# Token halves exchanged in half of the heads of an mLSTM kernel, so that the four quarters of TensorE's array get equal columns

## The chip, the cores and the metric

The kernel runs on one core of one Trainium2 chip. A core has a matrix engine (TensorE, PE in the profile, with PEld for its weight loads), VectorE (DVE), ScalarE (ACT), GpSimd (POOL), a queue that only issues transfers (SyncE, SP), and 16 DMA engines. The metric is the device time of one execution in microseconds; times below are the median of three runs.

## The reference

Two blocks follow each other. The first is an mLSTM cell, a recurrence with exponential gates over 768 tokens, for 4 batches and 8 heads of 40 dimensions:

```python
for t in range(S):
    m_new = np.maximum(f_gate[:, :, t] + m, i_gate[:, :, t])
    f_stab = np.exp(f_gate[:, :, t] + m - m_new)
    i_stab = np.exp(i_gate[:, :, t] - m_new)
    C = f_stab * C + i_stab * einsum('bhd,bhe->bhde', vt, kt)
    n = f_stab * n + i_stab * kt
    h_tilde, nq = einsum('bhde,bhe->bhd', C, qt), einsum('bhd,bhd->bh', n, qt)
    y[:, :, t] = sigmoid(o_gate) * h_tilde / np.maximum(np.abs(nq), 1.0)
```

The second, a mixture of depths, scores each token of the result (320 numbers), picks the 128 best of each batch, and adds a gated two-layer network for those alone:

```python
xe = x[b, top_idx]
ye = np.maximum(xe @ w1, 0.0) @ w2          # 320 -> 1024 -> 320
out[b, top_idx] = x[b, top_idx] + sigmoid(scores[b, top_idx])[:, None] * ye
```

## The kernel before

The recurrence is done in chunks. A tile is 128 tokens of one batch; there are 6 a batch, 24 in all, and `step(n)` handles tile n while it prepares tiles n+1 and n+2. Within a tile every pair of tokens (s, t) with s not after t gives a product k.q times a weight; earlier tiles come in through the state C.

For a tile, TensorE does this:

- `turn` (L314) transposes k and q, so that heads stand on partitions: two heads of 64 (40 used) fill the 128.
- `products` (L371) multiplies k by q. One head takes 64 rows of the array, and 64 tokens of k take 64 columns, so each product lies in one quarter of the array. For the first 64 tokens of k all 128 tokens of q are needed, for the last 64 only the last 64 of q, since the others come before them. Each matmul in float32 shows as two records.
- `weights` (L347, in the first tile L343 and L345) makes the exponents of the weights from two operands, a (from the input gate and the forget gate's sums) by k's token and M (a running maximum) by q's token. ScalarE takes their exponential (L348).
- `exchange` (L397, L403) applies the state C to q, and multiplies k by the weighted v, for the next state. `within` (L428) multiplies the weighted products P by v.

GpSimd's `causal` (L353) sets the weights of pairs in the wrong order to zero, in two selects of four heads each; in the first tile a matrix of large negative numbers, `never` (L332), does it instead. DVE multiplies products and weights to P (L377), adds the state's share to `within` (L433), makes the denominators (L437 to L441), and multiplies by the gate into x (L448), which is stored. GpSimd makes sor, the gate over the denominator (L443), wv, the weighted v (L360), and the decayed C (L385).

The gates come first. They lie as 96 rows (3 tiles, 4 batches, 8 heads) of 128 tokens, in two groups of three tiles. `sums` and `maxima` are scans on DVE (L194, L198). `split` (L230 to L233) cuts a row of float32 into three bfloat16 parts, which TensorE then spreads over partitions (pO: L272, L247): `split(g, 1, ...)` does a, `split(g, 0, ...)` does M. `scales` (L236, L237) makes the factors that weight v and the state, `columns` and `keep` turn them (L282, L287).

Each engine executes its instructions in the order in which the Python text issues them: that order is written out by hand, first for the tiles 0 to 3, then in `step`. So an instruction that waits holds up all that stand behind it on its engine. A transfer that ScalarE, SyncE or GpSimd issues stands in that engine's queue too. Transfers issued by SyncE and ScalarE share eight semaphores: each waits until the transfer that used its semaphore before, eight earlier, has landed.

Loads are issued four tiles ahead, at the start of a step, into five buffers. From step 8 on the network of the batch before is done in pieces in each step: `first` (L546), `second` (L570), and `enter` (L526), which transposes the rows that an indirect transfer (`gather`, L510) has fetched by the numbers that `number` (L503) makes. The weights w1 and w2 are loaded in six pieces, one a step after the steps 7 to 12. The last batch's choice, gather and network come after the last step, one behind the other.

The step's order around the network is this (L698 to L709):

```python
W[n + 2] = weights(*steps[n + 2]); hide(n + 2)   # hide: causal
layer(b, c)                                      # c == 1: layers[b - 2].second(3, 6)
if c == 1:
    picked[b - 1] = gather(b - 1, number(sel[b - 1], token))
elif c == 2:
    enter(b - 1)
```

Of the kernel before, what the change touches and what calls it, by code (L numbers as in the profile page):

```python
# [8 lines left out]
FP = mybir.dt.float32  # L9
BF = mybir.dt.bfloat16  # L10
# [11 lines left out]
def kernel(  # L22
# [61 lines left out]
    def load_gates(eng, dst, src, g):  # L84
        for c in range(3):
# [20 lines left out]
                            channel_multiplier=-1)  # L106
    ident_b = const.tile([128, 128], BF, name="ident_b")
# [14 lines left out]

    def load_qk(n):
        for j, src in enumerate((k, q)):
            load_heads(n, qk_t[n % NB][:, j, :, 0:D], src)

    def load_v(n):
        load_heads(n, v_t[n % NB][:, :, 0:D], v)
# [17 lines left out]

    def places(u, js=(0, 1)):
        for j in js:
            own, sign = ((0, -1.0), (3, 1.0))[j]
            for part in range(3):  # L150
                nc.gpsimd.tensor_scalar(out=place[j][u][:, part, :, own + part, :], op0=OP.mult, scalar1=sign, scalar2=None,
                                        in0=head[:, 16 * u:16 * u + 16].rearrange("p (g h) -> p g h", h=4))
# [6 lines left out]
    for j in range(2):  # L159
        nc.vector.tensor_reduce(out=of[:, j:j + 1], op=OP.add, axis=AX.XY,  # L160
                                in_=ident.rearrange("p (g x) -> p g x", x=32)[:, :, 12 * j:12 * j + 12])
    nc.vector.tensor_reduce(out=third, in_=ident[0:NR, 0:NR].rearrange("p (c h) -> p c h", h=BH), op=OP.add, axis=AX.X)
# [10 lines left out]
    a = [gate.tile([NR, L], FP, name=f"a{g}") for g in range(2)]  # L173
    m_in = [gate.tile([NR, 1], FP, name=f"m_in{g}") for g in range(2)]
# [22 lines left out]
    def maxima(g):  # L197
        nc.vector.tensor_tensor_scan(out=FM[g][:, 1], data0=ones, data1=a[g], initial=-BIG, op0=OP.mult, op1=OP.max)  # L198

# [27 lines left out]
    def split(g, j, eng, rows=slice(0, NR)):  # L227
        x, xs = (FM[g][rows, 1], a[g][rows])[j], [part[rows] for part in parts[j][g]]
        rest = gate.tile([NR, L], FP, name=f"rest{j}", bufs=2)[rows]
        eng.tensor_copy(out=xs[0], in_=x)  # L230
        eng.tensor_tensor(out=rest, in0=x, in1=xs[0], op=OP.subtract)
        eng.tensor_copy(out=xs[1], in_=rest)
        eng.tensor_tensor(out=xs[2], in0=rest, in1=xs[1], op=OP.subtract)  # L233

    def scales(g):
        nc.scalar.activation(out=wk[g], in_=a[g], func=AF.Exp, bias=nM[g], scale=1.0)  # L236
        nc.scalar.activation(out=r[g], in_=FM[g][:, 1], func=AF.Exp, bias=m_in[g], scale=-1.0)  # L237
# [90 lines left out]
    def masked(pools):  # L328

        pW = [pool.tile([128, 4, L], FP, name="pW", tag=tag) for pool, tag in pools]  # L330
        for p in pW:
            nc.tensor.matmul(p, never, ident_b.unsqueeze(1).to_broadcast([128, 4, L]), start=True, stop=False)  # L332
# [18 lines left out]
    def causal(W):  # L351
        for h0 in range(0, H, 4):
            nc.gpsimd.affine_select(out=W[:, h0:h0 + 4, :], in_=W[:, h0:h0 + 4, :], compare_op=OP.is_ge, fill=0.0, base=0,  # L353
                                    pattern=[[0, 4], [1, L]], channel_multiplier=-1)
# [9 lines left out]
    def products(T):  # L364
# [3 lines left out]
        for p in range(NP):  # L368
            for s, ts in zip(HALVES, (slice(0, L), HALVES[1])):
# [274 lines left out]
    def step(n):  # L644
# [52 lines left out]
        else:  # L697
# [7 lines left out]
            layer(b, c)  # L705
            if c == 1:
                picked[b - 1] = gather(b - 1, number(sel[b - 1], token))
            elif c == 2:
                enter(b - 1)  # L709
# [39 lines left out]
    maxima(0)  # L749
    split(0, 1, nc.gpsimd)  # L750
# [18 lines left out]
    split(1, 1, nc.gpsimd)  # L769
# [9 lines left out]
    maxima(1)  # L779
    stated(0)  # L780
# [12 lines left out]
    stated(1)  # L793
    iota_i = const.tile([128, K_], I32, name="iota_i")
# [9 lines left out]
    level(1, pm)  # L804
    split(1, 0, nc.gpsimd)
# [49 lines left out]
    for n in range(3, N):  # L855
# [6 lines left out]
        if 0 <= n - NT - 1 < 6:  # L862
            piece = n - NT - 1
# [80 lines left out]
```

## Time and profile before

| | |
|---|---|
| median of three runs | 182.86 us (182.71 to 184.8) |
| profiled execution | 184.28 us |
| its span, first to last instruction | 181.3 us, granted clock 0.998 |
| PE, PEld | 169.9 us (94%), 140.1 us (77%) busy |
| DVE, ACT, POOL | 135.8 us (75%), 102.1 us (56%), 105.8 us (58%) |
| DMA | 24.68 MB, 106,801 packets, 100,752 of them under 512 B |
| load of k, q, v or the gate of a tile | 160 KB each, 4.0 to 4.9 us from issue to landing (medians) |
| products L371 | 768 matmul records, half of 128 columns and half of 64 |
| causal L353 | 46 selects, 678 ns each in the mean |

In the profile a group names a line, an engine and an operation, then "out<-in"; `x48` is its count, and behind the bar stand the busy time, the mean of one in ns, and the time that the engine sat idle just before, with what ended most of that. In a timeline the first number is the start and the second the length, in us, and a bracket gives the idle time before and its releaser. SPq and ACTq are transfers issued by SyncE and ScalarE. In the chain each row is a start, a length and what the end of the program waited for at that time. A matmul's length includes the time in which it passes through the array, so the next one starts before it ends, and a busy PE isn't PE at its peak.

### The profile page before, as it was taken

What the parts mean: (1) busy time and instruction counts of PE and PEld (TensorE: products, weight loads), DVE (VectorE), ACT (ScalarE), POOL (GpSimd) and SP (SyncE); (2) the same over time, 40 slices, a digit from 0 to 9 for tenths busy, and PEclk for the clock granted to TensorE, in tenths of its full rate; (3) what the DMA queues carried; (4) which work ended last, traced back from release to release, by engine and by line L of the source; (5) the groups of instructions that cost most, each with busy time, mean ns of one, the idle gap of its engine ahead of it and who ended that gap; (6) DMA issues with size and microseconds to landing.
All of it is one profiled execution on the core that took longest, in us unless ns stands there. A gap on an engine that the chain in (4) does not pass through costs nothing.

```text
span 181.3 us, 7327 instructions
## 1 busy us (share of the span) xinstructions
PE 169.9 (94%) x2992; PEld 140.1 (77%) x2992; DVE 135.8 (75%) x403; ACT 102.1 (56%) x250; POOL 105.8 (58%) x176
## 2 busy tenths in 40 slices
PE   7989997999999999999989899999999999989990
PEld 2578976878777878889778598898878979869950
DVE  7767888898888875968996669698988788584120
ACT  3186869899998896466634454565535652201100
POOL 7987987778887992526854543655666361013202
PEclk9999999999999999999999999999999999999999
DMA  3999999999998999999999999889962101010100
GB/s 72 153 148 138 155 158 179 180 171 177 166 160 164 229 179 224 194 160 236 143 208 208 193 175 176 154 167 173 160 68 76 40 36 40 36 40 36 38 0 36
DMA packets 106801, 24.68 MB, mean 136 GB/s; under 512 B 100752, under 2 KB 106512, under 8 KB 106768
## 3 DMA queue, kind: packets, MB, share of 16 engines
q1 hardware_dynamic: 105952, 22.77, 77.6%
q0 software_dynamic: 384, 1.31, 2.5%
q8 instruction: 23, 0.38, 1.0%
q10 hardware_dynamic: 432, 0.15, 0.6%
q14 instruction: 10, 0.08, 0.2%
HBM read 19.63 MB, written 4.59 MB: 134 GB/s over the span
## 4 chain that ended last, share of the span: by engine, by line
PE 61%; issue 12%; ACT 10%; DMA 7%; POOL 5%; DVE 3%; POOLq 1%
PE pH L428 10%; PE ph L546 10%; PE pS L371 10%; PE pt L314 8%; PE pIC L397 5%; DMA xe<-out_dram,idx 5%; PE pIC L403 4%; PE pW L347 3%; PE py L570 3%; PE pS L190 3%; ACT W L348 2%; ACT M_o L258 2%; POOL W L353 2%; ACT T L315 2%; DMA out_dram<-ye,idx 2%
## 5 line engine op out<-in xcount | busy, mean ns | idle before, releaser
L443 POOL TENSOR_TENSOR sor<-so,rec 128x320 f32<-128x320 f32 x24 | 17.8, 740 | 36.7 <-DVE rec L441 32.7
L348 ACT ACTIVATE W<-pW 128x512 f32<-128x512 f32 x48 | 26.1, 598 | 20.8 <-PE pW L347 20.5
L377 DVE TENSOR_TENSOR P<-pS,W 128x512 f32<-128x512 f32 x48 | 30.9, 686 | 3.6 <-PE pS L371 1.6
L315 ACT COPY T<-pt 128x512 f32<-128x512 f32 x47 | 25.3, 589 | 12.8 <-PE pt L314 12.3
L353 POOL TENSOR_SCALAR_AFFINE_SELECT W<-W 128x512 f32<-128x512 f32 x46 | 30.2, 678 | 3.2 <-ACT W L348 3.2
L428 PEld LDWEIGHTS pH<-v,P 128*64 128x64 f32 x768 | 24.4, 138 | 8.6 <-DVE x L448 3.5
L428 PE MATMUL pH<-v,P 128*64 128x64 f32 x768 | 27.6, 225 | 2.5 <-issue 1.3
L471 DVE SCALAR_TENSOR_TENSOR ge<-sb,sc,earlier 128x128 bf16<-128x128 f32 (+5 forms) x23 | 18.1, 792 | 13.0 <-ACT sb L465 12.9
L371 PE MATMUL pS<-T 64*64 64x64 f32 (+1 forms) x768 | 26.2, 255 | 0.0
L314 PE MATMUL pt<-ident,qk 128*128 128x128 f32 x192 | 25.6, 276 | 0.2 <-ACT W L348 0.2
L314 PEld LDWEIGHTS pt<-ident,qk 128*128 128x128 f32 x192 | 21.1, 141 | 2.2 <-ACT W L348 0.4
L371 PEld LDWEIGHTS pS<-T 64*64 64x64 f32 x768 | 20.4, 132 | 1.9 <-issue 0.7
L570 PE MATMUL py<-w,hT 128*128 128x320 f32 x64 | 19.4, 444 | 0.5 <-DMA w<-in_moe_w_dram 0.5
L546 PE MATMUL ph<-xeT,w 128*128 128x128 f32 x144 | 18.1, 280 | 0.0
L546 PEld LDWEIGHTS ph<-xeT,w 128*128 128x128 f32 x144 | 16.7, 192 | 1.5 <-issue 1.5
L576 POOL DMA_INDIRECT out_dram<-ye,idx x4 | 4.6, 1140 | 20.2 <-DVE ye L574 20.2
L570 PEld LDWEIGHTS py<-w,hT 128*128 128x128 f32 x64 | 11.5, 191 | 5.7 <-issue 1.1
L397 PE MATMUL pIC<-C,T 128*64 128x82 f32 x320 | 15.2, 236 | 0.0
L360 POOL TENSOR_TENSOR wv<-v,cols 128x328 f32<-128x328 f32 x20 | 14.8, 742 | 0.0
L385 POOL TENSOR_TENSOR C<-C,cols 128x328 f32<-128x328 f32 x16 | 13.4, 835 | 0.1
L397 PEld LDWEIGHTS pIC<-C,T 128*64 128x64 f32 x320 | 12.7, 137 | 0.3 <-issue 0.2
L448 DVE TENSOR_TENSOR x<-pH,sor 128x320 f32<-128x320 f32 x24 | 11.6, 485 | 1.1 <-POOL sor L443 1.1
(166 smaller groups left out, 282.2 us busy)
## 6 DMA issues: line engine op xcount, KB each, us to landing
qk<-in_k_dram SPq DMA_DIRECT2D x24, 160.0 KB, 4.0
qk<-in_q_dram SPq DMA_DIRECT2D x24, 160.0 KB, 4.6
v<-in_v_dram SPq DMA_DIRECT2D x24, 160.0 KB, 4.9
so<-in_o_gate_dram SPq DMA_DIRECT2D x24, 160.0 KB, 4.4
out_dram<-x SPq DMA_DIRECT2D x24, 160.0 KB, 3.4
w<-in_moe_w_dram SPq DMA_DIRECT2D x2, 480.0 KB, 4.4
w<-in_moe_w_dram SPq DMA_DIRECT2D x2, 384.0 KB, 4.3
w<-in_moe_w_dram SPq DMA_DIRECT2D x4, 96.0 KB, 4.2
```

Source lines behind the costliest of these rows:

```text
L314: nc.tensor.transpose(pt[:, p, :], qk[:, j, 2 * p:2 * p + 2, :].rearrange("s a d -> s (a d)"), ident)
L315: copy(out=T[:, j], in_=pt)
L348: nc.scalar.activation(out=W[:, h0:h0 + 4, :], in_=pW, func=AF.Exp)
L353: nc.gpsimd.affine_select(out=W[:, h0:h0 + 4, :], in_=W[:, h0:h0 + 4, :], compare_op=OP.is_ge, fill=0.0, base=0, pattern=[[0, 4], [1, L]], ...
L371: nc.tensor.matmul(pS_t[j][s, p, ts], T[e, 0, p, s], T[e, 1, p, ts], start=True, stop=True)
L377: nc.vector.tensor_tensor(out=P[:, :, j, :], in0=pS[j], op=OP.mult, in1=W.rearrange("p (n a) t -> p n a t", a=2)[:, :, j, :])
L397: nc.tensor.matmul(pI[t, 2 * p * D1:2 * (p + 1) * D1], T[:, 1, p, t], C[:, p].rearrange("e a d -> e (a d)"), start=True, stop=True)
L428: nc.tensor.matmul(pH[t, 2 * p + j, :], P[:, p, j, t], v1[:, 2 * p + j, :], start=True, stop=True)
L443: nc.gpsimd.tensor_tensor(out=sor, in0=so, in1=rec.unsqueeze(2).to_broadcast([128, H, D]), op=OP.mult)
L471: nc.vector.scalar_tensor_tensor(out=ge[:, GE[u]:GE[u + 1]], in0=sb.rearrange("p t l -> p (t l)")[:, 0:n], scalar=sc[:, u:u + 1], in1=earl ...
L546: nc.tensor.matmul(self.ph[:, f % 4, :], w1[:, j, f * 128:(f + 1) * 128], self.xeT[:, j, :], start=(j == 0), stop=(j == NDC - 1))
L570: nc.tensor.matmul(self.py, self.hT[:, f, :], w2[:, f, :], start=(f == 0), stop=(f == NFC - 1))
```

## The change

For the heads 4 to 7, the rows of k, v and a hold the token halves exchanged: tokens 64 to 127 stand on partitions 0 to 63, and tokens 0 to 63 on partitions 64 to 127. In these heads it is then the second half of partitions that meets all 128 tokens of q, and the first half that meets 64.

In the diff HALVES are the slices 0 to 63 and 64 to 127, and NP is 4.

- k and v of a tile are loaded by three transfers each (`load_turned`) instead of one: heads 0 to 3 whole, and heads 4 to 7 by halves.
- `turn_halves` makes a_t from a: an activation with a row scale of one or zero (`side`: heads 0 to 3, heads 4 to 7), and two DVE operations that add the exchanged halves in the other rows. `split(g, 1)` and wk take a_t.
- `causal` is three selects instead of two: the heads 4 to 7 need one over 64 partitions and all tokens, and one over the other 64 partitions and 64 tokens. `never_t` is `never` with halves exchanged.
- `products` takes the pairs of heads in the order 0, 2, 1, 3, with 128 and 64 columns by halves as above.
- `split(1, 1)` moves from ahead of tile 0's P to behind tile 1's wv; the iotas that stood ahead of `split(1, 0)` move behind it.
- The weights' second and third piece come after step 8, and the others one step sooner than before.
- In the steps with c == 1 from the third batch on, `number` and `gather` stand between the second and the third of the step's three matmul blocks of `second`.

```diff
+    never_t = const.tile([128, L], BF, name="never_t")
+    for t, u in zip(HALVES, reversed(HALVES)):
+        nc.gpsimd.tensor_copy(out=never_t[:, t], in_=never[:, u])
...
+    def load_turned(n, dst, src):
+        b, c = n // NT, n % NT
+        by_token = src[b, :, c * L:(c + 1) * L, :].rearrange("h p d -> p h d")
+        nc.sync.dma_start(out=dst[:, 0:NP], in_=by_token[:, 0:NP])
+        for p, t in zip(HALVES, reversed(HALVES)):
+            nc.sync.dma_start(out=dst[p, NP:H], in_=by_token[t, NP:H])
+
     def load_qk(n):
-        for j, src in enumerate((k, q)):
-            load_heads(n, qk_t[n % NB][:, j, :, 0:D], src)
+        load_turned(n, qk_t[n % NB][:, 0, :, 0:D], k)
+        load_heads(n, qk_t[n % NB][:, 1, :, 0:D], q)
     def load_v(n):
-        load_heads(n, v_t[n % NB][:, :, 0:D], v)
+        load_turned(n, v_t[n % NB][:, :, 0:D], v)
...
+    side = const.tile([NR, 2], FP, name="side")
+    nc.vector.tensor_reduce(out=side, op=OP.add, axis=AX.XY,
+                            in_=ident[0:NR, 0:NR].rearrange("p (x y h) -> p y x h", y=2, h=NP))
...
+    def turn_halves(g):
+        nc.scalar.activation(out=a_t[g], in_=a[g], func=AF.Identity, scale=side[:, 0:1])
+        for t, u in zip(HALVES, reversed(HALVES)):
+            nc.vector.scalar_tensor_tensor(out=a_t[g][:, t], in0=a[g][:, u], scalar=side[:, 1:2], in1=a_t[g][:, t],
+                                           op0=OP.mult, op1=OP.add)
...
     def split(g, j, eng, rows=slice(0, NR)):
-        x, xs = (FM[g][rows, 1], a[g][rows])[j], [part[rows] for part in parts[j][g]]
+        x, xs = (FM[g][rows, 1], a_t[g][rows])[j], [part[rows] for part in parts[j][g]]
...
-        nc.scalar.activation(out=wk[g], in_=a[g], func=AF.Exp, bias=nM[g], scale=1.0)
+        nc.scalar.activation(out=wk[g], in_=a_t[g], func=AF.Exp, bias=nM[g], scale=1.0)
...
-        for p in pW:
-            nc.tensor.matmul(p, never, ident_b.unsqueeze(1).to_broadcast([128, 4, L]), start=True, stop=False)
+        for p, no in zip(pW, (never, never_t)):
+            nc.tensor.matmul(p, no, ident_b.unsqueeze(1).to_broadcast([128, 4, L]), start=True, stop=False)
...
     def causal(W):
-        for h0 in range(0, H, 4):
-            nc.gpsimd.affine_select(out=W[:, h0:h0 + 4, :], in_=W[:, h0:h0 + 4, :], compare_op=OP.is_ge, fill=0.0, base=0,
-                                    pattern=[[0, 4], [1, L]], channel_multiplier=-1)
+        for p, h0, base, n in ((slice(0, L), 0, 0, L), (HALVES[0], NP, -L // 2, L), (HALVES[1], NP, 0, L // 2)):
+            nc.gpsimd.affine_select(out=W[p, h0:h0 + 4, 0:n], in_=W[p, h0:h0 + 4, 0:n], compare_op=OP.is_ge, fill=0.0,
+                                    base=base, pattern=[[0, 4], [1, n]], channel_multiplier=-1)
...
-        for p in range(NP):
-            for s, ts in zip(HALVES, (slice(0, L), HALVES[1])):
+        for p in (0, 2, 1, 3):
+            for s, ts in zip(HALVES, (slice(0, L), HALVES[1]) if p < NP // 2 else (HALVES[1], slice(0, L))):
                 for j, e in enumerate(HALVES):
                     nc.tensor.matmul(pS_t[j][s, p, ts], T[e, 0, p, s], T[e, 1, p, ts], start=True, stop=True)
...
-            layer(b, c)
-            if c == 1:
+            if c == 1 and b > 1:
+                layers[b - 2].second(3, 5)
                 picked[b - 1] = gather(b - 1, number(sel[b - 1], token))
-            elif c == 2:
+                layers[b - 2].second(5, 6)
+            else:
+                layer(b, c)
+            if c == 2:
                 enter(b - 1)
...
     maxima(0)
+    turn_halves(0)
     split(0, 1, nc.gpsimd)
...
     sums(1, nc.gpsimd)
-    split(1, 1, nc.gpsimd)
     pads(4, nc.gpsimd)
...
     maxima(1)
+    turn_halves(1)
...
     stated(1)
+    split(1, 1, nc.gpsimd)
+    level(1, pm)
+    split(1, 0, nc.gpsimd)
     iota_i = const.tile([128, K_], I32, name="iota_i")
...
-    level(1, pm)
-    split(1, 0, nc.gpsimd)
     moving()
...
-        if 0 <= n - NT - 1 < 6:
-            piece = n - NT - 1
+        for piece in {7: (0,), 8: (1, 2), 9: (3,), 10: (4,), 11: (5,)}.get(n, ()):
             f0 = 3 * (piece % 3)
             (load_w1, load_w2)[piece // 3](slice(f0, min(f0 + 3, NFC)))
```

More of the change, by code (lines that the diff above doesn't have):

```diff
@@ L173 @@
     a = [gate.tile([NR, L], FP, name=f"a{g}") for g in range(2)]
+    a_t = [gate.tile([NR, L], FP, name=f"a_t{g}") for g in range(2)]
     m_in = [gate.tile([NR, 1], FP, name=f"m_in{g}") for g in range(2)]
```

## The prediction

> **What bounds the kernel now.** I read the cores view first (181.3 us, clock 0.998: nothing is throttled), then the page's chain, then the chain in order of time, then the timeline of single engines wherever the chain leaves TensorE.
>
> ```profile
> PE 61%; issue 12%; ACT 10%; DMA 7%; POOL 5%; DVE 3%; POOLq 1%
> L377 DVE TENSOR_TENSOR P<-pS,W 128x512 f32<-128x512 f32 x48 | 30.9, 686 | 3.6 <-PE pS L371 1.6
> L353 POOL TENSOR_SCALAR_AFFINE_SELECT W<-W 128x512 f32<-128x512 f32 x46 | 30.2, 678 | 3.2 <-ACT W L348 3.2
> ```
>
> TensorE holds 61% of the chain, but by stage it differs. Start to 35 us: TensorE with short waits. 35 to 52 us: ScalarE, back to back (T, W, M_o, so, scr). 55 to 64 us: DVE and GpSimd. 64 to 155 us: TensorE, step after step. Then a serial tail of 26 us, which the change doesn't touch. In the TensorE stretch a step looks like this (the chain in order of time):
>
> ```profile
> 104.04 1.08 PE pH L428 x32
> 105.13 0.57 PE pIC L397 x16
> 105.70 0.45 PE pIC L403 x16
> 106.14 1.02 PE pS L371 x24
> 107.16 0.32 PE pW L347 x2
> ```
>
> The k.q products take 1.02 us in every step, fixed. Three looks at the end of one such stage, in the timeline of TensorE, show why:
>
> ```profile
> 106.67 0.49 PE L371 MATMUL pS<-T 64*64 64x128 f32 x6
> ...
> 106.78 0.38 PE L371 MATMUL pS<-T 64*64 64x128 f32 x4
> ...
> 106.89 0.28 PE L371 MATMUL pS<-T 64*64 64x128 f32 x2
> ```
>
> Pairs start at 106.67, 106.78, 106.89: one quarter takes a 128-column matmul every 0.109 us. In the records the 64-column ones, which go to the other two quarters, are 0.058 apart and are all started by 106.69. So the two quarters of the first token half, with 8 records (4 products of two passes) of 128 columns each, set the 1.02 us; the others finish early.
>
> The last view is the start, on ScalarE's queue and DVE:
>
> ```profile
> 4.04 2.06 ACTq L87 DMA_DIRECT2D i_sb<-in_i_gate_dram  x3
> 7.64 0.27 ACT L275 CAST both_o<-pO 128x128 bf16<-128x128 f32 x1 [3.95 <-PE pO L272]
> ...
> 4.05 0.29 DVE L195 TENSOR_TENSOR a<-i_sb,FM 96x128 f32<-96x128 f32 x1
> 4.37 0.42 DVE L198 TENSOR_TENSOR_SCAN FM<-earlier,a 96x128 f32<-96x128 bf16 x1
> 4.82 0.21 DVE L230 CAST M<-FM 32x128 bf16<-32x128 f32 x1
> ```
>
> ScalarE issues gate DMAs until 6.10 us and computes nothing till 7.64. DVE goes straight from the scan to the split (4.82), whose product gives pO on TensorE at 7.10.
>
> **What the Trainium skill says.** "TensorEngine Tiling (Array Packing)", Key Properties: tiles operate independently. The trace agrees: different quarters start about 6 ns apart, one quarter every 109. "TensorE: Matmul & The Clock Gate", the table at its head: ScalarE's queue is strict FIFO. The trace agrees: the gate DMAs at 5.30 and 5.70 each started 0.02 after a landing they waited for. Same page, Part 1: after an idle window of about 3.4 us TensorE falls to half clock. No idle that long is in the trace; the largest gap is 1.28.
>
> **Part by part.** Durations are of the profiled execution: span 181.3, 184.28 in all, thus 2.98 around it and 1.42 above the median 182.86. I sum a difference and put it on the median.
>
> *Equal quarters.* Each quarter gets 4 records of 128 and 4 of 64 columns: 4 x 0.109 + 4 x 0.058 = 0.668 instead of 8 x 0.109 = 0.872, so 0.204 less per step. If instead the rate of issue limits (pIC L403: 16 in 0.45, so 0.028 each; 32 make 0.90) it is 0.12 less; I take 0.204.
> It counts where TensorE leads: products of tiles 10 to 23, starting at 66.2 to 150.7, except tiles 16 and 22. In those two steps the next pH waits for DVE's x (x ends 110.96, pH 111.06), whose queue ran from the 0.72 us wait for C without the products: nothing. 12 x 0.204 = 2.45. In the ScalarE stretch: nothing. At 55 to 64: nothing, since num, C and P fill DVE. In the start only tile 4's (33.2) still counts once GpSimd leads there (below): 0.2.
>
> *Weights and numbers sooner.* A stall of 0.52 on w at 93.5 goes. The numbers come two matmuls (0.57) earlier; but their gather stands behind GpSimd's selects, now three. Step 13: py from 93.2 instead of 94.0, numbers at 94.5, idx after P on DVE at 95.0, selects until 95.9, gather 95.9 instead of 96.48. It took 5.92 to land, so pX starts near 101.9 instead of 102.54: 0.6 gained, where two products (0.41) and the stall (0.52) offered 0.93. Net of the products counted: 0.2. On SP a weight piece (three DMAs) moves ahead of a later step's loads; those landed 5 us before use (k of tile 13: 74.0 against 82.4), so nothing.
>
> *Selects.* Two of 0.61 (1.22 a pair) become 0.61 + 0.61 (64 partitions, 512 elements; duration follows elements per partition) + a third of 256 elements, between 0.29 (L842, 128 elements) and 0.61; I take 0.38. GpSimd has 0.5 to 1.3 us idle in most steps. In step 8 it has none (58.0 to 63.6 is scr, C, W, xe, sor, then x and pH at 64.13): +0.4.
>
> *DMAs.* k and v go in three: nine issues a step instead of five, at 0.4 each (even 16 KB took 0.41) 3.6 us, within a step of 5 or more. Bytes are the same. Each waits for the landing of the one eight before, so at most 640 KB instead of 1,280 KB are under way; 160 KB land every 1.05 us, so that is 4.2 us of transfer against 3.12 from issue to landing of the first k: still fed. Bound: 0 to +1 us in the first steps, where q of tile 1 lands at 10.30 and is used at 11.2; the shift below covers it. I take 0.
>
> *turn_halves, the large term.* It is one ScalarE activation (0.39, as wk L236) and two DVE operations of 64 columns (between 0.17, L437, and 0.74, L261; 0.2 each), in front of both splits. In the built program's order the activation stands behind ScalarE's six gate DMAs. With the DMAs renumbered by the thirds of k, the last of these now waits for q of tile 0 (before: for a gate). That landed at 6.69; issued 0.9 later behind the same bytes, I take 6.7. Then 0.4 issue, 0.4 activation, 0.4 DVE: DVE's split starts at 8.05 instead of 4.82. Behind the waiting DVE instruction stand its split and carry, so pm and pO on TensorE; behind a_t stands GpSimd's split. **+3.2.** Cover: only ScalarE's idle 3.95, no cover for DVE. The side reduction (0.24) hides but for 0.07 in DVE's 0.17 wait; the two never_t copies (at most 0.3 each) precede GpSimd's wait for a.
>
> Then GpSimd falls further behind. Its view before:
>
> ```profile
> 12.95 0.78 POOL L360 TENSOR_TENSOR wv<-v,cols 128x328 f32<-128x328 f32 x1
> 13.73 1.22 POOL L353 TENSOR_SCALAR_AFFINE_SELECT W<-W 128x512 f32<-128x512 f32 x2
> ...
> 16.73 0.29 POOL L230 CAST M<-FM 96x128 bf16<-96x128 f32 x1 [0.75 <-DVE FM L224]
> ...
> 18.73 1.29 POOL L353 TENSOR_SCALAR_AFFINE_SELECT W<-W 128x512 f32<-128x512 f32 x2 [0.35 <-ACT W L348]
> ```
>
> After: wv at 16.1; selects from 17.1 (a_t1 is 0.4 ahead of the exponentials) to 18.7; wv to 19.4; split(1,1), moved here, 1.65 (10.41 to 12.05 before) to 21.05; split(1,0) 1.65 to 22.7; the iotas, moved behind it, 0.36; selects 1.6 to 24.7. They ended at 20.02: +4.7. P, x and pH of tile 1 follow (21.88 before). The next tile's selects had waited 0.56 for ScalarE, which is used up, and add 0.2: **+4.9** by 32 us. ScalarE's stretch follows TensorE (T at 35.10 waits for pt) and hands it on.
>
> **Sum.** 4.9 - 0.2 + 0.4 - 2.45 - 0.2 = +2.45. 182.86 + 2.45 = 185.3 (the profiled execution: 186.7).
>
> **Rivals.**
> - *The start is not held (not slower).* If q of tile 0 lands, or ScalarE is free, by 4.3, the exchange costs 0.6 for pO; the same GpSimd string from 13.5 ends its selects at 22.15, +2.1, +2.3 with the next. 2.3 - 0.2 + 0.4 - 2.65 = -0.15: 182.7. For it: a third of k is small. Against: q carries 160 KB behind k's and can't land before k, 5.28. Chance 0.2, with faster GpSimd strings in it.
> - *The clock falls (slower).* TensorE idles from 6.95 to 10.1, 3.15 us. From 3.4 on it would run at half clock for a window; 3.4 us of its gapless work up to the transposed columns (11.95) then takes 1.7 more, ahead of wv: 187.0. It decides if q lands after 6.95. Chance 0.17.
> - *The balance doesn't pay.* 0.12 or nothing per product: +1.0 or +2.45, 186.3 to 187.8. Against: the 58 ns of the short quarters. Chance 0.1.
> - *Faster by over 2%:* all products pay and nothing holds the start. Chance 0.03.
>
> **Numbers.** My forecast has 0.5; its own range is 184 to 187, by 0.5 of landing time, 0.2 per select string and 0.05 per product; about 0.08 of it lies above 186.5. Within 2% (about what a measurement can tell from no change): 0.2 + 0.42 + 0.05 of the balance rival = 0.67. Slower: 0.08 + 0.17 + 0.05 = 0.3. Range from just under the first rival to over the second: 181.9 to 188.1.
>
> **What would show it.** pS stages of 0.82; ScalarE's a_t near 7.1 right after its last gate DMA, DVE idle before it, pO near 10.3; GpSimd without idle from 16 to 25; pH of tile 1 near 26.6; pX in step 13 still waiting for xe. Wrong if a_t starts before 5, if pS stays at 1.0, or if TensorE's clock shows a dip near 10 us.

## The result and the profile after

The changed kernel takes 204.26 us (202.71 to 204.62), against 182.79 us for the kernel before beside it: 1.113 times as long, with an interval of 1.103 to 1.122. The forecast was 185.3 with a range of 181.9 to 188.1: it was wrong, and by an effect that it had put at nothing. Some executions of one kernel fall into a slower state, so ratios and intervals here compare fast executions alone, while a time is the median of all. The profiled execution took 204.19 us, with a span of 202.5 and a mean TensorE clock of 0.938.

From the page of the kernel after, the chain by engine and the two groups that answer to those shown before:

```profile
PE 42%; DVE 16%; POOL 10%; issue 10%; DMA 10%; SPq 6%; ACT 3%; POOLq 1%; ACTq 0%
L378 POOL TENSOR_SCALAR_AFFINE_SELECT W<-W 128x512 f32<-128x512 f32 (+2 forms) x69 | 41.2, 612 | 3.8 <-ACT W L372 2.2
...
L402 DVE TENSOR_TENSOR P<-pS,W 128x512 f32<-128x512 f32 x48 | 30.9, 685 | 7.7 <-POOL W L378 3.8
```

TensorE's part of the chain falls from 61% to 42%. SPq, SyncE issuing transfers, had no share before and has 6%. The selects take 11 us more in sum, and P now waits for them (3.8 us) where it had waited for TensorE's products.

The thing the change was built for came out as computed. The chain in order of time, in the stage where TensorE leads:

```profile
131.35 1.15 PE pH L453 x32
132.50 0.57 PE pIC L422 x16
133.07 0.81 PE pS L396 x24
133.89 0.34 PE pW L371 x2
```

The products pS take 0.81 instead of 1.02, where 0.82 was forecast.

The loss lies ahead of that stage. The starts of `within` (pH) of a tile, against the same tile before, are later by 9.7 us in tile 0, 11.4 in tile 4, 12.0 in tile 9, 17.5 in tile 10, 21.2 in tile 11, and 21.2 in tile 23. So 11.4 us are lost by tile 4, most of them before the first tile is done, 9 more in tiles 9 and 10, and from there on nothing. The two places, in turn:

The start, in the timelines of ScalarE, DVE and TensorE:

```profile
4.54 3.47 ACTq L87 DMA_DIRECT2D i_sb<-in_i_gate_dram  x3
8.05 0.40 ACT L219 ACTIVATE a_t<-a,side 96x128 f32<-96x128 f32 x1 [4.36 <-DMA qk<-in_q_dram]
...
8.49 0.48 DVE L221 SCALAR_TENSOR_TENSOR a_t<-a,side,a_t 96x64 f32<-96x64 f32 x2 [3.66 <-ACT a_t L219]
...
10.77 0.28 PE L240 MATMUL pm<-m,ident 32*32 32x3 f32 x6 [3.69 <-DVE m L234]
```

a_t waits for ScalarE's last gate transfer, which waits for q, as forecast, but q landed at 7.67 and not at 6.7. TensorE then stood idle for 3.69 us. What came of that is in the second part of the page, the granted clock in fortieths of the span (5.06 us each), in tenths:

```profile
PEclk9955589999999999979799999999999999999998
DMA  2677676756875677887889887857686873000200
```

A 5 is half clock: TensorE ran at it from 10.2 to 27.3 us. The line under it is the busy share of the DMA engines: 6 to 8 tenths. In the kernel before it is 9 almost throughout:

```profile
DMA  3999999999998999999999999889962101010100
```

The second place is tiles 9 and 10. TensorE's waits in the kernel after (total us, times, longest):

```profile
PE ph L571 <- DMA w<-in_moe_w_dram: 5.7, 3, 3.7
```

TensorE waits for w1, although the change issues it a step sooner in the program. The clock adds to the waits: behind the two long ones PEclk falls to half for 3.4 us each, which costs up to 1.7 us each, and 5.7 and 3.4 make up the 9 us. SyncE issued the first piece of w1 at 80.3 us, before at 60.0. In SyncE's timeline before, and after:

```profile
59.98 0.42 SPq L303 DMA_DIRECT2D w<-in_moe_w_dram  x1
...
80.35 0.43 SPq L327 DMA_DIRECT2D w<-in_moe_w_dram  x1
```

It stands behind 108 other transfers on SyncE's queue instead of 60: 48 more, four for each of the 12 tiles loaded ahead of it. A stretch of SyncE's timeline after:

```profile
42.59 0.53 SPq L131 DMA_DIRECT2D v<-in_v_dram  x1
43.21 1.27 SPq L133 DMA_DIRECT2D v<-in_v_dram  x2
44.62 0.51 SPq L125 DMA_DIRECT2D so<-in_o_gate_dram  x1
45.23 0.53 SPq L474 DMA_DIRECT2D out_dram<-x  x1
```

Two halves of 40 KB take 1.27 us to issue: 0.61 each and 0.05 between. The 160 KB of the output gates and of the store take no longer (0.51, 0.53). That SyncE is late by itself shows in the stores: x of tile 8 is ready at 76.04 and its store goes out at 87.37, before at 64.08 and 66.94. The DMA queues from 0.8 to 60 us (packets, bytes, rate; then the queue's time as a share of 16 engines), before:

```profile
DMA packets 50418, 9.35 MB, mean 158 GB/s; under 512 B 48998, under 2 KB 50406, under 8 KB 50406
...
q1 hardware_dynamic: 49974, 9.03, 103.9%
```

and after:

```profile
DMA packets 39328, 7.11 MB, mean 120 GB/s; under 512 B 38242, under 2 KB 39318, under 8 KB 39318
...
q1 hardware_dynamic: 38886, 6.83, 66.3%
```

Before, the DMA engines were full by this row, and there was little slack in them. (The row sums the time that packets took, and that grows with the load: from 30 to 58 us 173 GB/s made a share of 1.04 before, 127 GB/s one of 0.69 after. At the second ratio 173 would make 0.94, an estimate.) After, a third of the engines' time is idle, and a quarter of the bytes has not moved by 60 us. The Trainium skill names both limits ("Perfetto Trace Analysis", *What "DMA-bound" means*): the DMA engines, or the issuing sequencer when its track is solid with transfers. The two traces show one kernel on each side. The same page (*DMA Optimizations*) lets a split of transfers help if the engines are generally idle; at 103.9% they were not.

### The profile page after: what moved, and what is told of

It reads as the page before. It is cut to its first block, busy times and chain, and to the rows that moved or that the text cites. A ratio compares the mean times of both kernels' runs of the same rounds, so it can differ in the third digit from the quotient of the medians.

```text
span 202.5 us, 7545 instructions
## 1 busy us (share of the span) xinstructions
PE 177.2 (88%) x2992; PEld 146.7 (72%) x2992; DVE 137.3 (68%) x408; ACT 103.4 (51%) x252; POOL 116.2 (57%) x201
## 4 chain that ended last, share of the span: by engine, by line
PE 42%; DVE 16%; POOL 10%; issue 10%; DMA 10%; SPq 6%; ACT 3%; POOLq 1%; ACTq 0%
PE pH L453 8%; PE pt L338 6%; PE pS L396 6%; DVE P L402 5%; PE ph L571 5%; DVE ge L496 4%; PE pIC L422 3%; POOL W L378 3%; PE py L595 3%; PE pIC L428 3%; DMA w<-in_moe_w_dram 3%; SPq L133 2%; DMA v<-in_v_dram 2%; POOL scr L480 2%; PE pW L371 2%
## 5 line engine op out<-in xcount | busy, mean ns | idle before, releaser
L378 POOL TENSOR_SCALAR_AFFINE_SELECT W<-W 128x512 f32<-128x512 f32 (+2 forms) x69 | 41.2, 612 | 3.8 <-ACT W L372 2.2
L453 PEld LDWEIGHTS pH<-v,P 128*64 128x64 f32 x768 | 25.0, 140 | 14.6 <-DVE x L473 6.4
L496 DVE SCALAR_TENSOR_TENSOR ge<-sb,sc,earlier 128x128 bf16<-128x128 f32 (+5 forms) x23 | 18.4, 805 | 20.1 <-ACT sb L490 19.1
L338 PE MATMUL pt<-ident,qk 128*128 128x128 f32 x192 | 29.1, 301 | 0.2 <-ACT W L372 0.2
L338 PEld LDWEIGHTS pt<-ident,qk 128*128 128x128 f32 x192 | 24.2, 155 | 2.3 <-ACT W L372 0.4
L571 PE MATMUL ph<-xeT,w 128*128 128x128 f32 x144 | 20.8, 304 | 5.7 <-DMA w<-in_moe_w_dram 5.7
L571 PEld LDWEIGHTS ph<-xeT,w 128*128 128x128 f32 x144 | 18.9, 211 | 7.8 <-issue 6.8
L396 PE MATMUL pS<-T 64*64 64x64 f32 (+1 forms) x768 | 22.9, 260 | 0.0
L396 PEld LDWEIGHTS pS<-T 64*64 64x64 f32 x768 | 19.2, 140 | 2.5 <-issue 1.3
L595 PEld LDWEIGHTS py<-w,hT 128*128 128x128 f32 x64 | 11.4, 191 | 4.8 <-issue 1.4
L601 POOL DMA_INDIRECT out_dram<-ye,idx x4 | 4.6, 1140 | 17.5 <-DVE ye L599 13.2
L428 PE MATMUL pIC<-wv,qk 128*64 128x41 f32 x320 | 13.1, 230 | 0.3 <-issue 0.3
L458 DVE TENSOR_TENSOR pH<-num,pH 128x328 f32<-128x328 f32 x20 | 10.0, 499 | 4.7 <-PE pH L453 4.7
```

The costliest lines, as they stand in the source:

```text
L338: nc.tensor.transpose(pt[:, p, :], qk[:, j, 2 * p:2 * p + 2, :].rearrange("s a d -> s (a d)"), ident)
L378: nc.gpsimd.affine_select(out=W[p, h0:h0 + 4, 0:n], in_=W[p, h0:h0 + 4, 0:n], compare_op=OP.is_ge, fill=0.0, base=base, pattern=[[0, 4], [ ...
L396: nc.tensor.matmul(pS_t[j][s, p, ts], T[e, 0, p, s], T[e, 1, p, ts], start=True, stop=True)
L428: nc.tensor.matmul(pC[e, p, :], qk[:, 0, 2 * p + j, :], wv[:, 2 * p + j, :], start=True, stop=True)
L453: nc.tensor.matmul(pH[t, 2 * p + j, :], P[:, p, j, t], v1[:, 2 * p + j, :], start=True, stop=True)
L496: nc.vector.scalar_tensor_tensor(out=ge[:, GE[u]:GE[u + 1]], in0=sb.rearrange("p t l -> p (t l)")[:, 0:n], scalar=sc[:, u:u + 1], in1=earl ...
```

## The experiments

Each run stands beside the kernel before on the same chip. Theory S is that SyncE's issue time is what ran out; the other theories are named in each expectation.

### The split of the loads alone

Kernel before, with k and v of each tile in three transfers, nothing exchanged:

```diff
+    def load_parts(n, dst, src):
+        b, c = n // NT, n % NT
+        by_token = src[b, :, c * L:(c + 1) * L, :].rearrange("h p d -> p h d")
+        nc.sync.dma_start(out=dst[:, 0:NP], in_=by_token[:, 0:NP])
+        for p in HALVES:
+            nc.sync.dma_start(out=dst[p, NP:H], in_=by_token[p, NP:H])
...
-        for j, src in enumerate((k, q)):
-            load_heads(n, qk_t[n % NB][:, j, :, 0:D], src)
+        load_parts(n, qk_t[n % NB][:, 0, :, 0:D], k)
+        load_heads(n, qk_t[n % NB][:, 1, :, 0:D], q)
...
-        load_heads(n, v_t[n % NB][:, :, 0:D], v)
+        load_parts(n, v_t[n % NB][:, :, 0:D], v)
```

> The kernel before with k and v loaded by three transfers each (heads 0 to 3 whole, heads 4 to 7 by token halves, nothing exchanged), and nothing else changed. Theory S (SyncE's issues are the pace: one behind another takes about 0.65 us, whatever its size, and nine a step are 5.9 us): the first piece of w1 is issued near 80 us instead of 60, TensorE waits for w1 in steps 9 and 10, total 198 to 203 us. Rival L (the transfers keep up, as the prediction had it, and the loss of the changed kernel came from its start and its clock): total at most 185.

204.58 us, 1.109 (1.091 to 1.127). The first w1 piece went out at 78.3. TensorE's longest waits on transfers:

```profile
PE ph L553 <- DMA w<-in_moe_w_dram: 4.9, 4, 2.6
PE pt L321 <- DMA qk<-in_q_dram: 4.1, 5, 1.5
PE py L577 <- DMA w<-in_moe_w_dram: 2.7, 1, 2.7
```

The split alone, without a_t, selects or new products, gives the whole loss. TensorE waits for tiles of q too, not for the weights alone, and five of its waits are followed by 3.4 us at half clock (from 19.0, 53.2, 73.7, 83.9 and 107.8 us); the last two, behind waits for weights, add up to 1.7 us each to the loss.

Another rival is the eight shared semaphores, with fewer bytes under way when transfers are small. It doesn't hold SyncE here: wherever this trace tells the landing, from 12 us on the transfer eight before had landed at least 1.0 us before SyncE issued the next with its semaphore.

### The change with its loads whole

```diff
     def load_turned(n, dst, src):
-        by_token = src[b, :, c * L:(c + 1) * L, :].rearrange("h p d -> p h d")
-        nc.sync.dma_start(out=dst[:, 0:NP], in_=by_token[:, 0:NP])
-        for p, t in zip(HALVES, reversed(HALVES)):
-            nc.sync.dma_start(out=dst[p, NP:H], in_=by_token[t, NP:H])
+        load_heads(n, dst, src)
```

> The changed kernel with k and v loaded whole by one transfer each, so that nothing is exchanged in them (a and the weights still are: the heads 4 to 7 get a wrong result). Theory S: only the start is left (a_t behind ScalarE's gate transfers, which then wait for less: a_t near 6.1 us, TensorE's first pO near 9.3, no dip of the clock), and the products' gain; total 183 to 186. Rival L: the start and the clock are as in the changed kernel, total 194 or more.

192.87 us, 1.046 (1.024 to 1.067): above what was expected. pO came at 9.4, but TensorE ran at half clock to 27 us here too, after an idle time of only 2.07 us. From the page and TensorE's timeline:

```profile
PEclk9955569999999998899999999999999999999999
...
9.22 0.23 PE L236 MATMUL pm<-m,ident 32*32 32x3 f32 x6 [2.07 <-DVE m L230]
```

### The change with its start mended

The first operation of a_t goes to DVE, so that nothing of it stands behind ScalarE's transfers:

```diff
-        nc.scalar.activation(out=a_t[g], in_=a[g], func=AF.Identity, scale=side[:, 0:1])
+        nc.vector.tensor_scalar(out=a_t[g], in0=a[g], scalar1=side[:, 0:1], scalar2=None, op0=OP.mult)
```

> The changed kernel with a_t's first operation on DVE instead of ScalarE, so that it doesn't stand behind ScalarE's gate transfers. Both theories: a_t near 5.4, first pO near 8, no dip of the clock. Theory S: the issues up to the first piece of w1 are the same in number, w1 is issued near 80 again, and the 10 us won at the start are lost waiting for it: total 201 to 204. Rival L (start and issues add): total 193 to 196.

204.59 us, 1.109 (1.090 to 1.128). The start was mended: a_t from 4.7, pO at 7.3, no half clock at 10 us, tile 1 later by 5.7 instead of 10.4. And nothing was won: w1 went out at 80.7, and the end is as late. SyncE's queue, which nothing in the start holds up, decides when tiles and weights arrive; time won ahead of them is waited away. By tile 9, ahead of the weights, `within` is as late (12.1 us) as in the kernel after (12.0).

### Whole loads and the start mended, and the clock

Both edits together leave the exchange in a, the three selects, the products and the reordering:

> The changed kernel with both suspects out: k and v loaded whole (nothing exchanged in them, so the heads 4 to 7 get a wrong result), and a_t's first operation on DVE. What stays: the order and columns of the products, three selects, the exchange of a, the moves. If the start and the issues are all of the loss, what the prediction had for the rest remains: products 2.65 less, selects 0.4 more in step 8, GpSimd's string at the start 2 to 2.3 more: 181.5 to 184. Rival: a third loss of 3 us or more is hidden in it, total over 186.

187.43 us, 1.012 (1.007 to 1.017). Next, whole loads with the start left as the change has it, but TensorE kept busy while it waits for a_t:

```diff
-    warm(1)
+    warm(11)
```

> The kernel after with k and v loaded whole, as in the run with whole loads (192.87, half clock from about 9 to 26 us), and with more of the throw-away products that TensorE runs before its first real work, so that it is idle under 1 us until pm. The start's waits stay (a_t on ScalarE near 6.5, pO near 9.4). If TensorE's idle time ahead of pm brings the half clock: no dip, the start of pH of tile 0 some 3 to 4 us earlier than there, and 187 to 189.5. Rival (the dip comes of something else at the start): the same half clock to 26 us and 192 to 194.

187.37 us, 1.013 (1.009 to 1.016). TensorE is idle 0.53 us ahead of pm and the clock stays full:

```profile
PEclk9999999999999996999999999999999999999999
...
9.16 0.23 PE L236 MATMUL pm<-m,ident 32*32 32x3 f32 x6 [0.53 <-DVE m L230]
```

pO is as late as with whole loads alone (9.3 against 9.4), yet pH of tile 0 starts at 18.4 instead of 23.8 and the time falls by 5.5 us (by the two ratios, 1.046 and 1.013, by 6). So the half clock costs about 5.5 us, and that is nearly all of the difference between whole loads alone, which was timed only twice, and whole loads with the mended start. The wait for a_t itself, the largest term of the prediction, costs nothing that these times show; in the two profiled executions it is 1.6 us (pH of tile 23 at 160.1 against 158.4), where 3.2 was forecast for pO and 4.9 for what follows.

### Products alone, selects alone

Kernel before with the order and the columns of the new products, and nothing exchanged (the products of the exchanged heads are then those of other token pairs):

```diff
-        for p in range(NP):
-            for s, ts in zip(HALVES, (slice(0, L), HALVES[1])):
+        for p in (0, 2, 1, 3):
+            for s, ts in zip(HALVES, (slice(0, L), HALVES[1]) if p < NP // 2 else (HALVES[1], slice(0, L))):
```

> The kernel before with only the products in the new order and columns (the heads 4 to 7 get the wrong pairs, so a wrong result). If the prediction's gain is right: 12 steps of about 0.19, 2.0 to 2.7 us less. Rival: DVE and GpSimd take up the slack in the TensorE stretch too: 0 to 1 us less.

184.95 us, 0.991 (0.984 to 0.998): 1.65 us won. Steps led by TensorE get 0.19 us shorter each, as from tile 11 to 12 (5.39 to 5.20); there are fewer of them than were counted. From tile 15 to 16 and from 21 to 22 nothing changes (7.09 us in both kernels), as the prediction had said.

Kernel before with three selects in place of two:

```diff
-        for h0 in range(0, H, 4):
-            nc.gpsimd.affine_select(out=W[:, h0:h0 + 4, :], ...)
+        for p, h0, base, n in ((slice(0, L), 0, 0, L), (HALVES[1], NP, -L // 2, L), (HALVES[0], NP, 0, L // 2)):
+            nc.gpsimd.affine_select(out=W[p, h0:h0 + 4, 0:n], ...)
```

> The kernel before with three selects instead of two (heads 0 to 3, then heads 4 to 7 by partition halves of 64 and 128 tokens; nothing exchanged). As predicted: 0.4 more in step 8 and up to 0.5 at the start, 0.4 to 1.2 us more. Rival: GpSimd is close to the bound in many steps and each pays: 3 us more or over.

188.43 us, 1.020 (1.009 to 1.031): 3.7 us lost, where the sum had 0.4 and a share of the start. The page of that run:

```profile
L353 POOL TENSOR_SCALAR_AFFINE_SELECT W<-W 128x512 f32<-128x512 f32 (+2 forms) x69 | 41.3, 599 | 5.8 <-ACT W L348 1.6
```

The third select takes 0.50 in the mean (0.41 at least). In this execution it counts in the start (pH 2.4 us later by tile 4), around step 8 (0.9), and 0.5 each in four later steps (tiles 13, 16, 19 and 22): those where DVE or GpSimd lead, the very steps in which the balanced products win nothing. Products and selects sum to 2.05, and the run with whole loads and mended start measured 2.2. That isn't a test of the two alone: this run has the exchange of a and the new order of weights and numbers too, and the order alone saves some 1.6 us there (below), so something else in it costs about as much.

### How the split costs

Kernel before, k and v in two transfers of four heads each, on all partitions:

```diff
+        for h in (slice(0, NP), slice(NP, H)):
+            nc.sync.dma_start(out=dst[:, h], in_=by_token[:, h])
```

> The kernel before with k and v loaded by two transfers each (heads 0 to 3, heads 4 to 7, all 128 tokens). Theory S: seven issues with the store's are 4.6 us a step, below the step's 5.2: 183 to 186, with a small loss at most. Rival P (each further transfer costs in proportion, in the DMA engines or by its landing): half of what three transfers each cost, near 192 if those give 201.

186.51 us, 1.011 (0.990 to 1.032), the first w1 piece at 64.4: nearer to theory S than to its rival. Now three transfers by heads (six, one and one), also on all partitions:

```diff
+        for h in (slice(0, 6), slice(6, 7), slice(7, 8)):
+            nc.sync.dma_start(out=dst[:, h], in_=by_token[:, h])
```

> The kernel before with k and v loaded by three transfers each, split by heads (6, 1 and 1) over all 128 partitions, instead of by partition halves. Theory S (SyncE's time per issue, whatever its form): the same as thirds by halves, first piece of w1 issued near 78 us, total 203 to 206. Rival F (the form over 64 partitions is what is slow): at most 190.

198.24 us (196.49 and 199.98), beside 185.44; w1 at 71.9. Issues took 0.44 (k) and 0.53 (v) in the median, not 0.61. Between the two theories: with nine issues in a step more than half of the loss is there without the form on 64 partitions, and the rest comes with it.

Then k alone in three, v whole, which leaves seven issues in a step instead of nine:

```diff
-        for j, src in enumerate((k, q)):
-            load_heads(n, qk_t[n % NB][:, j, :, 0:D], src)
+        load_parts(n, qk_t[n % NB][:, 0, :, 0:D], k)
+        load_heads(n, qk_t[n % NB][:, 1, :, 0:D], q)
...
         load_heads(n, v_t[n % NB][:, :, 0:D], v)
```

> The kernel before with k of every tile in three transfers (first four heads; last four heads in two halves of 64 tokens, each at its own tokens) and v whole: seven issues a step on SyncE, all else as before. Theory S (SyncE's issue time runs out): two issues of 0.65 us fewer than with k and v in thirds, where nine filled 6.3 us a step; seven need 5.0, which the steps of tiles 1 to 10 (5.2 to 7.4) still hold. So not half of the loss but most of it goes: the first w1 piece is issued at 62 to 66 us (before 60.0, thirds of k and v 78.3), TensorE's wait for w is under 1.5 us, and the time is 3 to 6 us above the kernel before. Rival (each small transfer costs a fixed delay, wherever it stands): half of the loss stays, the first w1 piece at 68 to 70 us and 9 to 12 us above the kernel before.

194.80 us (190.52 to 196.23), beside 184.55, w1 at 70.6: what the rival said, half of the loss; a repetition below bears it out. Theory S in its simple form, no cost until the issues fill a step, fell. But the number alone doesn't decide either: the two halves by heads make seven issues a step too, 84 ahead of w1 as here, and lost 2.0 us (its interval reaches from -1.9 to 5.9). Together with the full engines of the kernel before, another reading stood open: while SyncE issues two small transfers in a row it feeds 40 KB each 0.65 us, 63 GB/s, where the engines had moved 158, so they run dry, and they have little slack to make it good; parts of 80 KB at 0.51 to 0.53 us an issue feed some 140 (estimates, with the gaps of 0.05). Then the order should count. The same seven transfers, with each small one behind a large one (PARTS are the three parts of k, and `load_part`, not shown, issues one):

```diff
+    def load_step(n, so):
+        for i in range(3):
+            load_part(n, qk_t[n % NB][:, 0, :, 0:D], k, *PARTS[i])
+            (lambda: load_heads(n, qk_t[n % NB][:, 1, :, 0:D], q), so, lambda: load_v(n))[i]()
...
-            load_qk(n)
-            load_v(n)
-            load_so(n)
+            load_step(n, lambda: load_so(n))
...
-        load_qk(n)
-        load_so(n - 1)
-        load_v(n)
+        load_step(n, lambda: load_so(n - 1))
```

> The kernel before with the thirds of k of the run before (v whole, seven issues a step), in another order from tile 1 on: first four heads of k, q, a half, output gates, the other half, v; so each 40 KB half stands behind a transfer of 160 KB instead of behind the other half. Theory C (a half takes 0.65 us of SyncE and holds 0.26 us of transfer, so the DMA engines run dry only where halves follow each other; the engines had no slack, 1.04 of their time between 30 and 58 us before): the seven issues, about 4.3 us, hide in the 5.2 us that 800 KB a step take at 1.05 us for 160 KB; first w1 piece at 60 to 65 us, 1 to 5 us above the kernel before. Rival F (each half costs its 0.7 to 0.8 us wherever it stands): as with the halves together, first w1 piece at 69 to 71, 9 to 12 us above.

190.06 us, 1.024 (1.019 to 1.029), w1 at 66.9. Less than together, but the last part of tile 1's k now came late, TensorE waited 1.63 us for it and fell to half clock, so the two readings were not cleanly apart. Spread from tile 4 on only (tiles 0 to 3 with the thirds together), with the order together once more on the same chip:

```diff
-        load_step(n, lambda: load_so(n - 1))
+        load_qk(n)
+        load_so(n - 1)
+        load_v(n)
```

> As with the thirds of k spread, but tiles 0 to 3 are loaded in the order of the thirds of k together, so that the start of TensorE is not held; from tile 4 on each half of k stands behind a transfer of 160 KB (first four heads, q, half, output gates, half, v). Theory C (the engines run dry only where the halves stand together): no shift of more than 2 us until the step of tile 6, first w1 piece at 62 to 66 us, 2 to 6 us above the kernel before. Rival F (each half costs the same wherever it stands): first w1 piece at 69 to 71 us, 9 to 12 above.

> The thirds of k together once more, beside the run before on the same chip: first w1 piece at 69 to 72 us and 9 to 12 us above the kernel before under either theory.

Spread: 189.93 us, 1.021 (1.006 to 1.035), w1 at 66.4. Together: 194.16 us, 1.049 (1.038 to 1.061), w1 at 70.6. The DMA share from 30 to 58 us (the second last number of the windows' line, after the granted clock), spread:

```profile
30.00:58.00 28.00, 26.41 (x590) 21.78 (x588) 23.44 (x68) 26.18 (x71) 21.71 (x34) 1.00 0.86 158
```

and together:

```profile
30.00:58.00 28.00, 24.00 (x500) 19.46 (x496) 21.64 (x60) 23.96 (x66) 19.71 (x29) 0.97 0.79 138
```

So the order counts: half of the loss comes back with the same transfers. Part of this, too, goes through the clock. In the run together TensorE waited for q of tile 8:

```profile
54.62 0.63 PE L321 MATMUL pt<-ident,qk 128*128 128x128 f32 x4 [2.38 <-DMA qk<-in_q_dram]
```

Then it ran at half clock for 6.8 us, up to 3.4 us of loss; spread, it had no such wait and no half clock there. With nine in a step (`load_step` in this order) the order does not count:

```diff
+        load_part(n, kn, k, *PARTS[0])
+        load_part(n, kn, k, *PARTS[1])
+        load_heads(n, qk_t[n % NB][:, 1, :, 0:D], q)
+        load_part(n, kn, k, *PARTS[2])
+        load_part(n, vn, v, *PARTS[0])
+        load_part(n, vn, v, *PARTS[1])
+        so()
+        load_part(n, vn, v, *PARTS[2])
```

> The kernel before with k and v in thirds (nine issues a step), from tile 1 on in the order: k's first four heads, a half of k, q, the other half, v's first four heads, a half of v, output gates, the other half. Theory C: nine issues take 0.65 each, 5.85 us a step, 0.65 more than the 5.2 us of transfer, so over the 13 tiles loaded before w1 8 us or somewhat more remain: first w1 piece at 68 to 72 us (78.3 with the halves together), 8 to 13 us above the kernel before. Rival F: first w1 piece at 77 to 79, 19 to 22 us above.

207.70 us, 1.117 (1.110 to 1.125), w1 at 79.1. That is what the rival said: here the order gave nothing. From 30 to 58 us SyncE issued 38 transfers, one per 0.74 us, as it did in the kernel after. At that rate nine need 6.6 us; the kernel before did a step's 800 KB in about 5.2 us (160 KB each 1.05). So nine were too many in both orders; seven would need 5.2 by the same rate (an estimate), which is just what there is, and there the order decided. This fits both findings; that the engines run dry behind the small transfers is argued from the rates, and no view shows it directly.

Last, the thirds alone with the small transfers of v moved to another queue, from tile 5 on (v of tiles 0 to 4 whole):

```diff
+        if n < NB:
+            load_heads(n, v_t[n % NB][:, :, 0:D], v)
+        else:
+            load_parts(n, v_t[n % NB][:, :, 0:D], v, nc.scalar)
```

> The kernel before with k of every tile in three transfers (the first four heads, then the last four in two halves of 64 tokens), all on SyncE; v of tiles 0 to 4 stays whole, and from tile 5 its first four heads go on SyncE and its two halves on ScalarE's queue. All other transfers, and what each holds, are those of the thirds alone; SyncE has seven a step to issue instead of nine. Theory S (SyncE's issue time is what runs out): about 1.3 us less issue time a step than with the thirds alone, the first w1 piece is issued at 64 to 68 us instead of 78.3 (before: 60.0), TensorE waits for w 1 us or less, and the time is 186 to 191, the rest being ScalarE's own issues in the stretch where it leads (35 to 52 us). Rival (the number of transfers under way at once, or the small transfers' landing, whoever issues them): the first w1 piece not before 73, and 196 or more.

202.70 us, 1.094 (1.083 to 1.106), w1 at 75.6: the rival's numbers, but not for the rival's reason. SyncE no longer fell behind the steps (w1 went out 0.2 us after tile 8's `within`, before 1.9 after it, with all thirds on SyncE 12.2 after it), and TensorE no longer waited for w1. But the loss had moved to ScalarE. Its timeline:

```profile
31.25 1.36 ACTq L128 DMA_DIRECT2D v<-in_v_dram  x2
32.66 1.07 ACT L325 COPY T<-pt 128x512 f32<-128x512 f32 x2 [10.35 <-DMA qk<-in_k_dram]
```

In the chain, the first of the moved transfers waits for the landing of wg, which SyncE had issued at 27.2 (the queues share their semaphores):

```profile
27.17 4.01 DMA wg<-in_moe_w_gate_dram
...
31.20 0.02 ACTq L128
```

ScalarE, done at 22.3, has its copies behind it. TensorE, idle for 7.9 us meanwhile, ran at half clock from 29.0 to 42.7. pH of tile 1 was later by 2.4, that of tile 2 is by 13.8. The skill says that balancing over issuing engines may help when issuing is the bound ("Perfetto Trace Analysis", *DMA Optimizations*); here it took away SyncE's delay and cost 11 us on the engine that was to help. As a test between S and its rival the run is therefore not clean.

## Why the prediction was wrong, point by point

- **The step that failed is "*DMAs*"**: "nine issues a step instead of five, at 0.4 each", 3.6 us, "within a step of 5 or more", "still fed", and the term taken as 0. An issue took 0.6, not 0.4: the row of 0.41 was for 16 KB gate transfers issued at the start of the queue. With gaps and waits it was 0.74, so 6.6 us instead of 3.6, more than the 5.2 of a step. And "still fed" was argued from the bytes under way, when the row of the DMA engines, at 9 tenths nearly throughout, said that there was little room to make an idle moment good. Its 3.12 us from issue to landing was that of the first load, into idle engines, where the medians are 4.0 to 4.9; but the transfers under way weren't what ran out. The bound of one microsecond came from the first steps alone. Measured: +20.8 for the split alone. The loads were held to be early ("landed 5 us before use"), and the weights behind them were not looked at again: a lead of 5 us is spent in a few steps of 1.4.
- *The sum as a form.* Adding terms failed for start and loads: 20.8 for the split, 5.4 for the start, 2.2 for the rest, but 21.5 in all. That products and selects add up to what the rest measured (2.05 against 2.2) is partly luck, since the rest holds other terms. The queue of loads runs beside the engines, and the later of the two counts.
- *turn_halves.* The mechanism was right, place and all: a_t behind ScalarE's gate transfer, that behind q, DVE and pO behind a_t. Its size was off twice. q was forecast at 6.7 and came at 7.67, since two half transfers ahead of it took 0.71 and 0.61 to issue; pO came at 10.97 instead of 10.3. And once the clock holds the wait by itself costs nothing that the times show, 1.6 us between two profiles.
- *The clock, a rival at 0.17.* It came, and its condition (q after 6.95) was met; but that condition isn't the right one, since with whole loads it came after 2.07 us idle too. Its price of 1.7 us for one window was too small: half clock lasted 17 us, and with whole loads it cost 5.5. It isn't what decides, though: without it (the mended start) the change is as slow.
- *Equal quarters.* 0.81 per step, as computed; 1.65 us instead of 2.65, since fewer steps are led by TensorE alone.
- *Selects.* 0.50 in the mean for the third in the kernel after, 0.38 forecast. Where it counts was misjudged: 3.7 us instead of 0.4 and a share of the start. Idle time of GpSimd in a step was taken for cover; P waits for the select that comes last, and idle time elsewhere in the step doesn't bring that forward.
- *Weights and numbers sooner.* In the run with whole loads and mended start, tile 13 to tile 15 takes 12.11 us instead of 14.00, and 13.75 with the products alone: about 1.6 us for the order, where the sum had 0.2. pX no longer waits for xe there, which the prediction had said it still would. The kernel after shows it as well (12.35), but it can't make up for w1 being 20 us late two steps earlier.

## What to carry to other kernels

Before a transfer is split, look at two rows: the busy share of the DMA engines, and how long the issuing queue takes for one transfer as it stands in that queue, not at an idle start. If the engines are full and the issues of a step come near the step's time, each small transfer is paid for at its issue time, and what stands last in the queue (here the weights) is late by the sum. Of the splits tried here, equal parts on all partitions cost least. If small ones must be, and the issues still fit into the step, put each behind a large one, and don't move them into the queue of an engine that computes without looking at what they wait for.

## What the runs showed of the hardware

- A 40 KB transfer on 64 partitions took 0.61 us to issue (at least 0.60), and the 160 KB one behind it 0.60 where 0.37 had been seen; on 128 partitions parts of 20 to 120 KB took 0.44 to 0.53 in the median. Why the half on 64 partitions takes longer isn't settled.
- Half clock came in whole pieces of 3.4 us, one or more on end. After 3.69 and 2.07 us idle at the start there were five (17.1 us), after 1.63 three, though by the profile TensorE was busy nearly throughout; around 7.9 us idle four, elsewhere one or two. The idle time just before doesn't decide alone: one piece followed 1.32 us idle in the run kept busy (at 70.1 us) and 0.84 in the split alone (at 19.0), none followed 1.50 in the two halves by heads, nor 1.28 in the kernel before. The skill ("TensorE: Matmul & The Clock Gate", Part 1) gives a window of about 3.4 us for both directions. The length of the pieces agrees with it; but less than such a window idle was enough here, and the return took up to 17 us: the measurement decides. What the return waits for, no run shows.
- A select of 512 elements took 0.70 on 64 partitions and 0.63 on 128 in the kernel after, and one of 256 elements on 64 partitions 0.50 (means); with three selects alone it was 0.66, 0.64 and 0.50. Halving the partitions saved nothing, and halving the elements about a quarter.
